# Attention and mixture of experts on one core: an emptying of GpSimd's queue in the last slot, and its halves multiplied and stored one by one

## The chip, the cores and the metric

The kernel runs on one core of a Trainium2 chip. The metric is the device time of one execution in microseconds, as the median of several runs; lower is better. The core has five engines that run side by side: TensorE (PE: matmuls, with its weight loads shown apart as PEld), VectorE (DVE), ScalarE (ACT), GpSimd (POOL) and SyncE (SP). They wait for each other through semaphores. An engine's name with a q (POOLq) stands for its sequencer, which issues, waits and branches.

## The reference, cut to what matters

Attention with rotary positions over 8 batches, 8 heads, 576 positions and 64 values a head gives 4608 tokens of 512 values. Each token then goes through the one expert of eight that its gate picks, and is scaled:

```python
x = attn_out.transpose(0, 2, 1, 3).reshape(N, D)            # N = 4608, D = 512
logits = x @ w_gate
e_idx = np.argmax(logits, axis=1)
probs = softmax(logits); gate_w = probs[np.arange(N), e_idx]
eom = 1.0 / (1.0 + np.exp(-(x @ w_output_gate)))
for e in range(E):                                          # E = 8
    mask = e_idx == e
    h = np.maximum(x[mask] @ w1[e], 0.0)                    # w1[e]: 512 x 1024
    ye = h @ w2[e]                                          # w2[e]: 1024 x 512
    out[mask] = gate_w[mask, None] * eom[mask, e, None] * ye
```

## The kernel before, in words

The first part computes the attention; the second (class `Moe`) does the experts. Tokens of one expert are gathered into *slots*. A slot has one expert and one or two *halves* of 128 tokens; `self.todo[s][0]` is the number of halves. The order of the slots is fixed when the program is built: full slots of two halves first, then slots of two halves and of one mixed. The last slot that always runs has two halves; some further slots stand in a branch (`tc.If`, L1237) that is taken only if the tokens need them, which they do not here.

`run` (L1225) calls `slot` (L1202) for each slot. `slot` has eight steps j. In steps 0 to 3, `first` (L1125) multiplies the tokens with a quarter of w1 (matmuls at L1121, or L1113 in a slot of one half), and ScalarE and VectorE turn the sums into the hidden rows `ht`, kept as a high and a low part (L1137, L1138). In steps 4 to 7, `second` (L1152) multiplies them with a quarter of w2 into one accumulator `py` a half (matmuls at L1163): for each of the two blocks f of a quarter it goes over the halves and makes three products (high x high, high x low, low x high). In every step, weights of later steps are loaded by SyncE (L1069) and split into a high and a low part (ScalarE L1078; VectorE L1080, now and then GpSimd). Step 6 gathers the tokens of the slot after the next (GpSimd, an indirect DMA, L1055). In step 7, `store` (L1166) scales `py` of half 0 on ScalarE (L1172) and that of half 1 on VectorE (L1174) into `y`, and GpSimd scatters each half to the token rows of `out` with an indirect DMA (L1175). For the last slots no later weights, tokens or turns are left to prepare, so in the last slot steps 4 to 7 hold nothing but `second` and `store`.

Each engine runs its instructions in the order in which the program names them; the framework adds the semaphore waits between instructions that touch the same memory. Two scatters both write to `out` at rows that are known only at run time, so each scatter waits until the one before it has landed.

Behind the last slot stands the branch: each engine loads the flag `used` (L1235) and jumps over the body (L1237), and GpSimd's INC_SWDGE_SEM (L1237) stands there too. At the end of the program (recorded under L1273, the line that opens the framework's context) SyncE waits for the semaphores of all engines and DMAs, each engine runs a DRAIN, and GpSimd gathers the others' answers and releases them. At the program's start (L1285) there is a DRAIN on each engine as well.

Of the kernel before, what the change touches and what calls it, by code (L numbers as in the profile page):

```python
# [10 lines left out]
F32 = mybir.dt.float32  # L11
# [3 lines left out]
AF = mybir.ActivationFunctionType  # L15
ALU = mybir.AluOpType
# [5 lines left out]
DM = H * D  # L22
E, FF = 8, 1024
P = 128
# [562 lines left out]
def place(tc, pools, pairs, b, NT, cc, trib, oneb, cnt, xbs, xd, row, lists, later):  # L587
# [173 lines left out]
    if last:  # L761
        later += [lambda i=i: store(i) for i in range(3)]
        run = lambda *fs: lambda: [f() for f in fs]
        return [s0, run(s1, s2), s3, run(s4, s5), run(s6, s7), run(s8, add0), both(s9, 1), lambda: [add(c) for c in (2, 3, 4)],
                run(s10, s11, s12), run(s13, base), no, no, no, no, s14, no, s14b, run(s15, s16, s17)] + [
                lambda c=c: (ones(c), places(c)) for c in range(NCH)] + [no, no, s20, no, s21, no]
# [12 lines left out]
    if b == NT // S - 2:  # L779
        later += [lambda i=i: store(i) for i in range(3)]  # L780
        fs += [(22, 2, s13)]
    else:
        fs += [(29, 2, lambda: gated(0, 2)), (33, 2, lambda: store(0)), (38, 2, lambda: gated(2, NCH)),
               (42, 2, lambda: store(1)), (42, 2, lambda: store(2))]
# [3 lines left out]
class Moe:  # L788
# [360 lines left out]
        self.nc.scalar.copy(hth[:, js, 0:P], tp[:, 0:2, :])  # L1149
        self.nc.vector.tensor_tensor(out=htl[:, js, 0:P], in0=tp[:, 0:2, :], in1=hth.bitcast(F32)[:, js, 0:P], op=ALU.subtract)  # L1150

    def second(self, s, j):  # L1152
        hth, htl = self.ht[s]
        K = self.todo[s][0]
        if j == 0:
            self.pys[s] = [self.pm.tile([P, DM], F32, tag=f"py{h}", name=f"py{s}_{h}{self.nm}") for h in range(K)]
        py = self.pys[s]
        for f in (2 * j, 2 * j + 1):
            wh, wl = (a.rearrange("p (f d) -> p f d", d=DM)[:, f % 2, :] for a in self.wp[8 * s + 4 + j])
            for h in range(K):  # L1160
                hs = slice(h * P, h * P + P)
                for n, (st, mv) in enumerate(((hth, wh), (hth, wl), (htl, wh))):
                    self.nc.tensor.matmul(py[h], st[:, f, hs], mv, start=(f == 0 and n == 0), stop=(f == 7 and n == 2))  # L1163
        self.wp.pop(8 * s + 4 + j)

    def store(self, s):  # L1166
        nc = self.nc
        py, gs = self.pys.pop(s), self.gss.pop(s)
        y = self.buf("y", s, 2, 0, [P, 2, DM], F32, f"y{s}{self.nm}")
        for h in range(self.todo[s][0]):  # L1170
            if h == 0:
                nc.scalar.activation(y[:, 0, :], py[0], AF.Copy, scale=gs[:, 0:1])  # L1172
            else:
                nc.vector.tensor_scalar(y[:, 1, :], py[1], gs[:, 1:2], None, op0=ALU.mult)  # L1174
            nc.gpsimd.indirect_dma_start(  # L1175
                out=self.out, out_offset=bass.IndirectOffsetOnAxis(ap=self.ids(s, h), axis=0),
                in_=y[:, h, :], in_offset=None, bounds_check=self.NT - 1, oob_is_err=False)

    LOADS, SPLITS, LEAD = 8, 9, 6

# [18 lines left out]
        for u in range(8 * s + 3, 8 * s + self.LEAD):  # L1199
            self.split(u)  # L1200

    def slot(self, s, left, per=2):  # L1202
        for j in range(8):
            u = 8 * s + j
            single = self.todo[s][0] == 1
            if j < 4:
                if s or j > 1 or not self.n0:
                    self.first(s, j)
            else:
                self.second(s, j - 4)  # L1210
            if single and 1 <= j <= 4:
                self.across(s, j - 1)
            self.split(u + self.LEAD)
            self.load(u + self.LOADS)
            if j in (4, 5):
                self.turn(s + 1, j - 4)
            if j == 7:
                self.store(s)
            if j == 6:
                self.gather(s + 2)  # L1220
            for _ in range(per if s or j > 1 else 1):
                if left:
                    left.pop(0)()

    def run(self, left):  # L1225
        left = list(left)
        N = self.end
        self.more(0)
        for s in range(N):
            self.slot(s, left)  # L1230
        while left:
            left.pop(0)()
        M = len(self.todo)
        if N < M:
            rv = self.nc.values_load(self.used[0:1, 0:1], min_val=0, max_val=self.n1,  # L1235
                                     skip_runtime_bounds_check_because="bounded by the number of tokens")
            with self.tc.If(rv > self.T):  # L1237
                self.begin0(N, M, "b")
                self.begin1(N)
                self.more(N)  # L1240
                for s in range(N, M):
                    self.slot(s, [])
# [46 lines left out]
```

## Time and profile before

| what | us |
|---|---|
| median of 3 runs (lowest, highest) | 986.09 (985.11, 987.06) |
| the profiled execution: its time | 985.03 |
| the profiled execution: span from first to last instruction | 983.3 |
| busy in the span: PE, DVE, ACT, POOL | 898.3, 759.7, 629.1, 563.4 |
| mean granted TensorE clock, share of full | 0.993 |

The times of the runs are what the change is judged by. The span is what the trace covers; all times of instructions below count from its start. Of the profiled execution's time, 1.7 us lie outside the span. A POOL row of DMA_INDIRECT is the issue of an indirect DMA, not its transfer; the transfer ends when it lands, which the chain of waits shows as DMA.

### The profile page before, as it was taken

To read this page: it belongs to the slowest core of one execution; us is meant where nothing else is said; L and a number is where in the kernel's file an instruction comes from. 1 tells how busy PE (TensorE), PEld (TensorE's weight loads), DVE (VectorE), ACT (ScalarE), POOL (GpSimd) and SP (SyncE) were. 2 spreads that over 40 slices of the span, in tenths; PEclk is the share of its full clock that TensorE was granted. 3 is DMA by queue.
4 is the path that set the end of the run, shared out by engine and by line. 5 is a ranking of instruction groups with operands and counts; after the bars stand their busy time and mean duration, and the time that the engine had idled before them with its cause. 6 is when DMAs were issued, how large, how long until landed. Compare 5 with 4: busy or idle time off the path is not lost.

```text
span 983.3 us, 34130 instructions
## 1 busy us (share of the span) xinstructions
PE 898.3 (91%) x14413; PEld 780.4 (79%) x14413; DVE 759.7 (77%) x1322; ACT 629.1 (64%) x1278; POOL 563.4 (57%) x565
## 2 busy tenths in 40 slices
PE   4989888988989888988899999999999999999993
PEld 3777777767777777776688989999899999988993
DVE  6889998998999999998779766557766766667560
ACT  4676787876878778686654544457656656565460
POOL 5787899999999999998411212142504234050410
PEclk9999999999999999999999999999999999999997
DMA  6543454564555456353589867667876869678630
GB/s 231 195 174 129 187 222 144 201 239 145 202 203 190 165 195 236 130 212 110 185 309 286 315 221 237 222 221 266 305 239 241 302 195 336 203 248 291 216 107 20
DMA packets 57822, 208.39 MB, mean 212 GB/s; under 512 B 7946, under 2 KB 8252, under 8 KB 57664
## 3 DMA queue, kind: packets, MB, share of 16 engines
q1 hardware_dynamic: 49920, 183.78, 53.7%
q0 software_dynamic: 6464, 21.26, 5.8%
q8 instruction: 115, 1.88, 0.8%
q10 hardware_dynamic: 1280, 1.11, 0.3%
q14 instruction: 43, 0.35, 0.1%
HBM read 186.06 MB, written 22.43 MB: 212 GB/s over the span
## 4 chain that ended last, share of the span: by engine, by line
PE 57%; DVE 14%; POOL 14%; issue 5%; ACT 4%; DMA 4%; SPq 0%; POOLq 0%; DVEq 0%; ACTq 0%
PE py L1163 18%; PE ph L1121 17%; PE acc L550 8%; PE sc L504 7%; DVE pm L513 6%; POOL raw L455 5%; DVE pt L528 4%; POOL kq L468 4%; PE ph L1113 3%; POOL raw L459 2%; ACT pm L520 2%; DVE xb L577 2%; PE mtp L1086 2%; DVE wl L1080 1%; POOL pl L738 1%
## 5 line engine op out<-in xcount | busy, mean ns | idle before, releaser
L520 ACT ACTIVATE pm<-pm,m 128x576 f32<-128x576 f32 x288 | 221.5, 770 | 96.2 <-DVE pm L513 94.2
L1080 DVE TENSOR_TENSOR wl<-wr,wh 128x1024 fp32r<-128x1024 f32 x172 | 216.0, 1270 | 37.5 <-ACT wh L1078 35.6
L513 DVE TENSOR_SCALAR_CACHE_REDUCE pm<-sc 128x576 f32<-128x576 f32 x288 | 207.7, 754 | 33.2 <-PE sc L504 26.1
L550 PE MATMUL acc<-pt,v 32*64 32x160 f32 (+1 forms) x9216 | 197.6, 295 | 18.6 <-DVE xb L577 6.9
L1163 PE MATMUL py<-wh,ht 128*128 128x512 f32 x640 | 213.1, 399 | 0.0
L1121 PE MATMUL ph<-xt,wh 128*128 128x256 f32 x1088 | 195.5, 282 | 0.5 <-DVE xt L1102 0.5
L550 PEld LDWEIGHTS acc<-pt,v 32*64 32x64 f32 x9216 | 157.4, 131 | 44.4 <-issue 22.0
L1078 ACT CAST wh<-wr 128x1024 fp32r<-128x1024 f32 x184 | 187.9, 1049 | 0.0
L528 DVE STREAM_TRANSPOSE pt<-pm 128x1152 f32<-128x1152 f32 x128 | 175.7, 1373 | 0.0
L1121 PEld LDWEIGHTS ph<-xt,wh 128*128 128x128 f32 x1088 | 167.8, 188 | 3.5 <-DVE xt L1102 2.2
L504 PE MATMUL sc<-kq 64*128 64x288 f32 x1536 | 149.8, 318 | 18.1 <-ACT kq L465 9.4
L455 POOL TENSOR_TENSOR raw<-raw,rt 128x1152 f32<-128x1152 f32 x62 | 164.3, 2651 | 0.6
L504 PEld LDWEIGHTS sc<-kq 64*128 64x128 f32 x1536 | 115.1, 190 | 47.7 <-issue 16.2
L1121 PE MATMUL ph<-xt,wl 128*128 128x256 f32 x544 | 152.8, 281 | 0.0
L1163 PEld LDWEIGHTS py<-wh,ht 128*128 128x128 f32 x640 | 120.3, 188 | 24.1
L1163 PE MATMUL py<-wl,ht 128*128 128x512 f32 x320 | 125.0, 391 | 0.0
L1175 POOL DMA_INDIRECT out<-y,2idx x24 | 28.2, 1174 | 168.3 <-ACT y L1172 122.8
L1137 ACT ACTIVATE ht<-ph 128x512 fp32r<-128x512 f32 x68 | 40.7, 598 | 108.7 <-PE ph L1121 108.7
L1121 PEld LDWEIGHTS ph<-xt,wl 128*128 128x128 f32 x544 | 102.5, 188 | 0.2
L1138 DVE SCALAR_TENSOR_TENSOR ht<-ph,ht 128x512 fp32r<-128x512 f32 x68 | 47.0, 691 | 69.1 <-ACT ht L1137 69.1
L468 POOL TENSOR_TENSOR kq<-raw,kq 128x1152 fp32r<-128x1152 f32 (+1 forms) x33 | 82.7, 2507 | 9.4 <-ACT kq L465 9.4
L459 POOL TENSOR_TENSOR raw<-raw 128x1152 f32<-128x1152 f32 (+1 forms) x33 | 82.5, 2499 | 1.8
(247 smaller groups left out, 1055.5 us busy)
## 6 DMA issues: line engine op xcount, KB each, us to landing
wr<-in_w SPq DMA_DIRECT2D x184, 512.0 KB, 4.9
raw<-in_qk SPq DMA_DIRECT2D x64, 576.0 KB, 4.9
v<-in_v SPq DMA_DIRECT2D x64, 576.0 KB, 6.8
xd<-xb SPq DMA_DIRECT2D x16, 640.0 KB, 4.4
xd<-xb SPq DMA_DIRECT2D x8, 160.0 KB, 5.0
rt<-in_rope ACTq DMA_DIRECT2D x1, 576.0 KB, 5.5
xg<-xd,2idx POOLq DMA_INDIRECT x24, 6.9
out<-y,2idx POOLq DMA_INDIRECT x24, 4.5
```

The costliest lines, as they stand in the source:

```text
L455: self.eng(eng).tensor_tensor(out=rv, in0=rv, in1=rt, op=ALU.mult)
L459: self.eng(eng).tensor_tensor(out=r, in0=r, in1=self.sides(self.raw, t, 1, x), op=ALU.add)
L468: self.eng(eng).tensor_tensor(out=self.sides(self.kq, t, 0, x), in0=self.sides(self.raw, t, 0, x), in1=self.sides(self.kq.bitcast(F32), t, ...
L504: self.nc.tensor.matmul(self.ps[i][:, a, :HS], st, self.kq[r, mov, x], start=(n == 0), stop=(n == 2))
L513: self.nc.vector.tensor_scalar(self.halves(i), self.ps[i][:, :, :HS], 1.0, FAR, op0=ALU.mult, op1=ALU.min, accum_out=self.m[i])
L520: self.nc.scalar.activation(self.pc[i], self.pc[i], AF.Exp, bias=self.m[i], scale=-1.0, accum_out=self.z[:, zi:zi + 1])
L528: self.nc.vector.transpose(out=self.pt[:, c:c + 6:5, :], in_=self.pc[units])
L550: nc.tensor.matmul(self.acc[h * D:h * D + D, a, o:o + 32 * n], self.v[r, h, j, :], self.pt[r, u:u + n, 32 * j:32 * j + 32], start=(j == 0) ...
L1078: self.nc.scalar.copy(wh, r)
L1080: eng.tensor_tensor(out=wl, in0=r, in1=wh.bitcast(F32), op=ALU.subtract)
L1121: nc.tensor.matmul(ph[:, f, :], st[:, dc, fs], mv[:, dc, :], start=(n == 0), stop=(n == 11))
L1163: self.nc.tensor.matmul(py[h], st[:, f, hs], mv, start=(f == 0 and n == 0), stop=(f == 7 and n == 2))
```

## The change

A method `close` takes the place of the last four calls of `second` and of `store` in the last slot that always runs: it makes all products of half 0 (all four quarters of w2), scales it on ScalarE and scatters it, then the same for half 1, also on ScalarE. `second` gets the list of halves to work on, and keeps the weights until `close` drops them. The second scatter of that slot is declared free of a dependence on the first. At the end of step 0 of the last slot, GpSimd gets a `drain` instruction. Other slots keep their order.

```diff
-    def second(self, s, j):
+    def second(self, s, j, halves=None):
...
-        if j == 0:
+        if s not in self.pys:
...
-            for h in range(K):
+            for h in range(K) if halves is None else halves:
...
-        self.wp.pop(8 * s + 4 + j)
+        if halves is None:
+            self.wp.pop(8 * s + 4 + j)
+
+    def scatter(self, s, h, y):
+        return self.nc.gpsimd.indirect_dma_start(
+            out=self.out, out_offset=bass.IndirectOffsetOnAxis(ap=self.ids(s, h), axis=0),
+            in_=y[:, h, :], in_offset=None, bounds_check=self.NT - 1, oob_is_err=False)
...
+    def close(self, s):
+
+        before = None
+        for h in range(self.todo[s][0]):
+            for j in range(4):
+                self.second(s, j, (h,))
+            if h == 0:
+                py, gs, y = self.pys[s], self.gss.pop(s), self.buf("y", s, 2, 0, [P, 2, DM], F32, f"y{s}{self.nm}")
+            self.nc.scalar.activation(y[:, h, :], py[h], AF.Copy, scale=gs[:, h:h + 1])
+            st = self.scatter(s, h, y)
+            if before is not None:
+                self.tc.declare_no_dep(st.ins, before.ins, reason="a token is in one half of one slot: the rows are others")
+            before = st
+        self.pys.pop(s)
+        for j in range(4):
+            self.wp.pop(8 * s + 4 + j)
...
-    def slot(self, s, left, per=2):
+    def slot(self, s, left, per=2, last=False):
...
-            else:
+            elif not last:
                 self.second(s, j - 4)
...
-                self.store(s)
+                self.close(s) if last else self.store(s)
             if j == 6:
                 self.gather(s + 2)
+            if j == 0 and last:
+                self.nc.gpsimd.drain()
...
-            self.slot(s, left)
+            self.slot(s, left, last=s == N - 1)
```

## Rows read from the trace of the kernel before

**Rows 1.** The page: engines' busy time; chain that ended last, by engine.

```profile
PE 898.3 (91%) x14413; PEld 780.4 (79%) x14413; DVE 759.7 (77%) x1322; ACT 629.1 (64%) x1278; POOL 563.4 (57%) x565
...
PE 57%; DVE 14%; POOL 14%; issue 5%; ACT 4%; DMA 4%; SPq 0%; POOLq 0%; DVEq 0%; ACTq 0%
```

**Rows 2.** Stretches: length, busy of PE PEld DVE ACT POOL, clock, DMA share, GB/s.

```profile
957.20:968.40 11.20, 11.19 (x50) 8.90 (x49) 0.69 (x1) 1.27 (x2) 0.00 (x0) 1.00 0.01 1
...
968.40:983.30 14.90, 0.00 (x0) 0.00 (x0) 0.75 (x1) 0.02 (x1) 1.96 (x2) 0.62 0.09 32
...
949.10:963.80 14.70, 14.70 (x101) 13.59 (x100) 5.22 (x6) 4.19 (x6) 0.00 (x0) 1.00 0.04 13
...
975.30:981.90 6.60, 0.00 (x0) 0.00 (x0) 0.00 (x0) 0.00 (x0) 0.00 (x0) 0.50 0.00 0
```

**Rows 3.** The chain that ended last, in order of time: start, us, what.

```profile
947.02 3.67 DMA out<-y,1idx
...
968.69 3.15 DMA out<-y,2idx
```

**Rows 4.** GpSimd in order of time, from 946: start, us, instruction, idle before.

```profile
947.02 2.06 POOL L1175 DMA_INDIRECT out<-y,1idx  x1 [7.42 <-ACT y L1172]
...
968.69 0.98 POOL L1175 DMA_INDIRECT out<-y,2idx  x1 [19.61 <-ACT y L1172]
...
972.62 0.98 POOL L1175 DMA_INDIRECT out<-y,2idx  x1 [2.94 <-DMA out<-y,2idx]
```

**Rows 5.** ScalarE and VectorE in order of time, last slot.

```profile
967.73 0.69 ACT L1172 ACTIVATE y<-py,gs 128x512 f32<-128x512 f32 x1 [9.66 <-PE py L1163]
...
953.40 1.22 DVE L1080 TENSOR_TENSOR wl<-wr,wh 128x1024 fp32r<-128x1024 f32 x1 [0.25 <-ACT wh L1078]
...
958.10 0.69 DVE L1138 SCALAR_TENSOR_TENSOR ht<-ph,ht 128x512 fp32r<-128x512 f32 x1 [2.13 <-ACT ht L1137]
...
968.42 0.75 DVE L1174 TENSOR_SCALAR y<-py,gs 128x512 f32<-128x512 f32 x1 [9.63 <-PE py L1163]
```

**Rows 6.** Line 1237 from 972: ns min/median/max, first and last start.

```profile
L1237 POOLq INC_SWDGE_SEM  x1: 1839/1839/1839, 973.3 to 973.3; - x1
```

**Rows 7.** The program's end, line 1273, by instruction: ns, first and last start.

```profile
L1273 SPq DRAIN  x2: 7/10/13, 975.8 to 975.9; - x2
...
L1273 POOLq DRAIN  x1: 6773/6773/6773, 975.2 to 975.2; - x1
...
L1273 POOLq EVENT_SEMAPHORE  x4: 17/17/17, 982.0 to 983.2; - x4
...
L1273 POOLq DRAIN  x2: 46/150/254, 982.5 to 983.0; - x2
...
L1273 DVEq DRAIN  x2: 10/14/17, 969.4 to 982.3; - x2
```

**Rows 8.** TensorE in order of time: a slot of one half, the last slot.

```profile
944.02 0.39 PE L1163 MATMUL py<-wl,ht 128*128 128x512 f32 x1
...
944.71 0.39 PE L1163 MATMUL py<-wl,ht 128*128 128x512 f32 x1
...
957.27 0.39 PE L1163 MATMUL py<-wh,ht 128*128 128x512 f32 x1
...
967.99 0.40 PE L1163 MATMUL py<-wh,ht 128*128 128x512 f32 x1
```

**Rows 9.** Scatters to out from 900 on: from issue to landing.

```profile
DMA to landing us min/median/max: 2.6/3.7/5.8
```

**Rows 10.** The program's start, line 1285, GpSimd's DRAIN.

```profile
L1285 POOLq DRAIN  x1: 184/184/184, 0.3 to 0.3; - x1
```

**Rows 11.** MOVEs, one ahead of each indirect DMA: scatters, gathers, index lists.

```profile
L1175 POOLq MOVE  x40: 29/29/29, 498.7 to 968.5; - x40
...
L1055 POOLq MOVE  x40: 29/29/38, 466.5 to 923.7; - x40
...
L857 POOLq MOVE  x2: 29/29/29, 549.4 to 596.3; - x2
```

More of the change, by code (lines that the diff above doesn't have):

```diff
@@ L1163, in second @@
                     self.nc.tensor.matmul(py[h], st[:, f, hs], mv, start=(f == 0 and n == 0), stop=(f == 7 and n == 2))
-        self.wp.pop(8 * s + 4 + j)
+        if halves is None:
[4 more added lines that the diff above has]
+            in_=y[:, h, :], in_offset=None, bounds_check=self.NT - 1, oob_is_err=False)
     def store(self, s):
-        nc = self.nc
         py, gs = self.pys.pop(s), self.gss.pop(s)
@@ L1171, in store @@
             if h == 0:
-                nc.scalar.activation(y[:, 0, :], py[0], AF.Copy, scale=gs[:, 0:1])
+                self.nc.scalar.activation(y[:, 0, :], py[0], AF.Copy, scale=gs[:, 0:1])
             else:
[L1174 to L1177, printed above, removed]
+                self.nc.vector.tensor_scalar(y[:, 1, :], py[1], gs[:, 1:2], None, op0=ALU.mult)
+            self.scatter(s, h, y)
+    def close(self, s):
[13 more added lines that the diff above has]
+            self.wp.pop(8 * s + 4 + j)
     LOADS, SPLITS, LEAD = 8, 9, 6
```

## The prediction

> **What bounds the kernel now.** I read the page first: TensorE is busy for most of the span and the chain that ended last runs mainly through it [rows 1], so what the change can win lies where TensorE no longer sets the pace. The table of stretches shows where that is [rows 2]: TensorE is full up to 968.4, the end of the last slot's second step, and does nothing in the last 14.9 us. From 975.3 to 981.9 no engine is busy and no DMA moves a byte. Next I read the tail. The chain of waits [rows 3] and GpSimd's order of time [rows 4] show that the first scatter of the last slot starts at 968.69, lands 3.15 us later, and only then the second starts, at 972.62, though its half was scaled by 969.17 [rows 5]. After it stands a fixed sequence on GpSimd: the skipped branch with INC_SWDGE_SEM, 1.84 us from 973.3 [rows 6], and a DRAIN from 975.2 that lasts 6.77 us [rows 7]. SyncE has its waits behind it at 975.9; GpSimd, which gathers the others at the end, first answers at 982.0 [rows 7]. So two things set the end: a wait of one scatter for the other, and a DRAIN that runs with every transfer landed.
>
> **The stores.** Step two of the last slot is 48 matmuls, whose starts run from 957.27 to 967.99 [rows 8]: 10.72 us over 47 gaps, 0.228 us each. The change keeps all 48 and puts the 24 of half 0 first. Does the new order stall TensorE? A slot of one half already puts its matmuls into one accumulator with no other half between, and starts three of them in 0.69 us there, 944.02 to 944.71 [rows 8], the same pace. The operands are needed earlier: those of the last weight unit at the 19th matmul instead of the 37th, so at 957.27 + 18 x 0.228 = 961.4 instead of 965.5. The last split of weights starts at 953.40 and takes 1.22 us, the last split of the hidden rows starts at 958.10 and takes 0.69 us [rows 5]: 954.6 and 958.8, 2.6 us before 961.4. The new order therefore costs nothing; without that cover TensorE would wait.
>
> Half 0 then ends at 957.27 + 23 x 0.228 + 0.40 = 962.9. ScalarE has nothing between 958.1 and 967.7 [rows 5], takes its 0.69 us and ends near 963.6; from ScalarE's end to the scatter it is 0.27 us now (968.42 to 968.69) [rows 4, 5], so scatter 0 starts near 963.9, 4.8 us earlier. It lands 2.6 to 5.8 us after its issue, median 3.7 [rows 9]: 966.5 to 969.7. Half 1 ends with TensorE at 968.39, as before. Its scaling moves from VectorE (0.75 us) to ScalarE (0.69 us), 968.43 to 969.12, and scatter 1 starts at 969.39 instead of 972.62: 3.23 us sooner. That the wait between the two is dropped is worth nothing at the median landing (967.6, 1.8 us early), and about 0.3 us of wait plus the 0.8 us from landing to scatter [rows 3, 4] if scatter 0 took the longest. What follows on GpSimd, SyncE's last waits included, hangs on scatter 1 and its landing and moves with it: **3.23 us**.
>
> **The emptying.** Where it stands, GpSimd has issued the scatter of 947.02, done at 949.08, and has nothing until the new scatter 0 [rows 4]: 14.8 us of cover. Only the two scatters are queued behind it, and nothing else waits for GpSimd in this slot. What does it do to the DRAIN at the end? Rows bound that one's later price. Below: a DRAIN with little or nothing ahead of it takes 0.18 us at the program's start and 0.05 to 0.25 us right behind the long one [rows 7, 10]. Above: 6.77 us, if the long one's price does not depend on what was emptied before. Between the ends stands an estimate: 82 indirect DMAs, 40 scatters, 40 gathers and 2 of index lists, are issued before it [rows 11], and (6.77 - 0.18) / 82 = 0.080 us each. I take this, because the long DRAIN outlasts every transfer, so it is work done on a list and not a wait for data, and the short ones stand where that list is empty. The new DRAIN in the slot then retires 80 of them, 0.18 + 80 x 0.080 = 6.6 us, from 949.1 to about 955.7, or until the scatter before it lands, 3.67 us after 947.02 [rows 3], whichever is later; 8.2 us remain before scatter 0. The last DRAIN has two left: 0.34 us. Then SyncE answers last, 0.7 us after the DRAIN starts (975.2 to 975.9) [rows 7], so a last DRAIN up to that length is free. GpSimd's answer moves from 982.0 to just behind 975.9, allowing 0.05 us for the signal: **6.05 us** more.
>
> **Sum.** 3.23 + 6.05 = 9.28 us. The profiled execution took 985.03 us for a span of 983.3, so its own time becomes 975.75. It lies 1.06 us under the median of the three runs shown, 986.09; against that the forecast is **976.8 us**. A measurement of this kernel tells apart about 0.2%, 2.0 us.
>
> **The rivals.** (1) *The price stays.* The last DRAIN costs 6.77 us whenever an indirect DMA ran before it, and the one in the slot is paid in the shade for nothing. Then only the stores gain: 986.09 - 3.23 = 982.9. For it: the trace has no second DRAIN behind an indirect DMA. Against: the transfers had landed before it began, so its length is not that of the last scatter. The Trainium skill, VectorE: DVE Perf Modes, section "The DRAIN you can't avoid", counts DRAINs around the program as boilerplate of a constant 12 ns or so on all five engines. By that rule there is nothing at the end to take away, and the sum would be that of the stores alone, 982.9. The trace agrees for SyncE and VectorE, 7 to 17 ns, and contradicts it for GpSimd, 6,773 ns [rows 7, 10].
>
> (2) *Part of the price stays*, since only the latest entries, or INC_SWDGE_SEM, carry it. Each microsecond of the last DRAIN beyond 0.7 gives one back: 976.8 to 982.9, middle 979.9.
>
> (3) *No change*: the 80 entries take much longer in the slot than at the end, and hold both scatters. Scatter 0 is late once the emptying exceeds 963.9 - 949.1 = 14.8 us; scatter 1 (at least 1.2 us behind, by scatter 0's 0.98 us [rows 4] and an issue) is late from 19.1 us, and the whole gain is gone at 28 us, 986.1. For it: GpSimd slows beside VectorE's splits, 2.06 us for a scatter at 947.02 against 0.98 later [rows 4]. Against: VectorE has only 5.2 us of work in that stretch [rows 2], and doubling the whole gives 13.2 us, still covered.
>
> (4) *Slower*: the emptying acts as a fence for all engines. TensorE then stands for its 6.6 us at the head of the slot, and if the last DRAIN stays too, the sum is 986.09 - 3.23 + 6.6 = 989.5. It decides for slower only when both hold; if the last one shrinks, it is 986.09 - 9.28 + 6.6 = 983.4. Against: the change adds one GpSimd instruction and no work of another engine that reads what GpSimd writes in this slot.
>
> That the change does not take the wait between scatters away at all would not show, as said: scatter 0 has mostly landed by then.
>
> **How the numbers follow.** The forecast has 0.65, the price that stays 0.15, a part of it 0.12 and the fence that still gains 0.01: faster 0.93. Rival 3 and other ways to land within 0.2% have 0.04, slower 0.03. The likeliest case alone spans 975.4 to 978.5: the runs shown scatter by 1 us either way, and 0.7 us lies on the last landing (2.6 or 3.2 us). The range reaches to the rival that keeps the price, with half a microsecond: 975.4 to 983.4, leaving out some 5% below and about 11% above.
>
> **What the profile after should show.** A DRAIN on GpSimd of 6 to 7 us from about 949; scatter 0 near 963.9 and scatter 1 near 969.4, with no wait for a landing between; two scalings of 0.69 us on ScalarE; TensorE still ending near 968.4; a last DRAIN under 0.7 us and a span near 974.0. The prediction is wrong if the last DRAIN is again several microseconds long, if the one in the slot lasts past 963.9, or if TensorE stops between 957 and 968.

## The result and the profile after

The changed kernel takes 977.13 us (median of 4 runs, 976.42 to 978.65) against 985.63 us beside it. The ratio is 0.9914 with a 95% interval of 0.9896 to 0.9931: 8.5 us less, 6.8 to 10.3. The forecast was 976.8 us, 9.28 us under the kernel before.

The profiled execution is the slowest of the four (978.65 us, span 976.9), and TensorE ends in it at 970.93, 2.5 us later than before [rows 8]. Those 2.5 us are lost far ahead of the change, on the way from the attention to the slots, where this execution has a stretch with the clock at its lower level (1.2 GHz). (Columns: length, busy time of PE, PEld, DVE, ACT and POOL with instruction counts, granted clock, DMA share, GB/s.)

```profile
470.00:520.00 50.00, 44.45 (x725) 39.14 (x724) 32.97 (x64) 29.62 (x54) 11.65 (x24) 0.93 0.59 215
```

A mean clock of 0.93 over 50 us is what 7 us at the lower level make. TensorE had been busy for all of the 5 us before the clock fell (470 to 475) and for 3.00 of the 5 us in which it fell. None of the seven experiments' executions below shows it there (1.00 in each). So kernels are compared here by their *tail* too: from the end of the last matmul to the end of the span. It was 983.3 - 968.39 = 14.9 us and is 976.9 - 970.93 = 6.0 us.

GpSimd in order of time (start, length, instruction, idle time before it and what ended it), to be held against [rows 4]:

```profile
949.50 2.06 POOL L1168 DMA_INDIRECT out<-y,1idx  x1 [7.41 <-ACT y L1177]
...
966.40 0.98 POOL L1168 DMA_INDIRECT out<-y,2idx  x1 [14.85 <-ACT y L1190]
...
971.93 0.98 POOL L1168 DMA_INDIRECT out<-y,2idx  x1 [4.54 <-ACT y L1190]
```

Scatter 0 starts 4.53 us before TensorE's end and scatter 1 1.00 us behind it, where it was 4.23 us; what released it is ScalarE's scaling and no longer a landing. ScalarE, against [rows 5]:

```profile
965.44 0.69 ACT L1190 ACTIVATE y<-py,gs 128x512 f32<-128x512 f32 x1 [4.91 <-PE py L1163]
...
970.97 0.69 ACT L1190 ACTIVATE y<-py,gs 128x512 f32<-128x512 f32 x1 [4.84 <-PE py L1163]
```

TensorE's second step of the last slot, first and last matmul; then three stretches around the emptying and the end (columns as above):

```profile
959.73 0.40 PE L1163 MATMUL py<-wh,ht 128*128 128x512 f32 x1
...
970.53 0.40 PE L1163 MATMUL py<-wh,ht 128*128 128x512 f32 x1
```

```profile
949.30:958.20 8.90, 8.90 (x78) 8.90 (x77) 5.68 (x7) 3.67 (x5) 2.06 (x1) 1.00 0.05 20
...
958.20:970.90 12.70, 12.70 (x63) 10.36 (x61) 0.93 (x2) 1.28 (x2) 0.98 (x1) 1.00 0.06 23
...
970.90:976.90 6.00, 0.03 (x1) 0.00 (x0) 0.00 (x0) 0.69 (x1) 0.98 (x1) 0.74 0.10 37
```

The 48 matmuls still take 10.80 us from first start to last, against 10.72, and TensorE is busy in every microsecond from the emptying's start to its own end: 8.90 of 8.90 and 12.70 of 12.70. So the emptying is no fence. The instructions of the emptying (line 1242), of the skipped branch (1259) and of the program's end (1295), against [rows 6, 7] (ns min/median/max, first and last start in us):

```profile
L1242 POOLq DRAIN  x1: 8903/8903/8903, 949.3 to 949.3; - x1
...
L1259 POOLq INC_SWDGE_SEM  x1: 246/246/246, 972.6 to 972.6; - x1
...
L1295 SPq EVENT_SEMAPHORE  x14: 17/28/2003, 972.8 to 976.8; - x14
...
L1295 POOLq EVENT_SEMAPHORE  x4: 17/17/17, 975.6 to 976.8; - x4
...
L1295 POOLq DRAIN  x3: 52/261/2148, 972.9 to 976.6; - x3
```

The last scatter, from issue to landing:

```profile
L1168 POOL DMA_INDIRECT out<-y,2idx x1: 982/982/982, 971.9 to 971.9; - x1
...
DMA to landing us min/median/max: 3.0/3.0/3.0
```

The DRAIN in the slot is recorded from 949.3, ahead of the scatter of 949.50 that stands before it, and ends at 958.2: 6.6 us behind the end of that scatter's issue. At the program's end two rows have shrunk, not one: the last DRAIN from 6,773 to 2,148 ns and INC_SWDGE_SEM from 1,839 to 246 ns. SyncE now stands 2,003 ns in one of its waits, for the last scatter's landing, and has its last waits behind that. The last DRAIN, too, ends only at 975.0, just behind the landing (971.9 + 3.0 = 974.9). GpSimd answers at 975.6, 3.7 us behind the issue of scatter 1, where it was 9.4 us.

### The profile page after: what moved, and what is told of

It is laid out like the page before. It is cut to its first block, busy times and chain, and to the rows that moved or that the text cites. A ratio compares the mean times of both kernels' runs of the same rounds, so it can differ in the third digit from the quotient of the medians.

```text
span 976.9 us, 34128 instructions
## 1 busy us (share of the span) xinstructions
PE 899.7 (92%) x14413; PEld 782.2 (80%) x14413; DVE 759.0 (78%) x1321; ACT 629.7 (64%) x1279; POOL 559.4 (57%) x565
## 4 chain that ended last, share of the span: by engine, by line
PE 56%; POOL 19%; DVE 12%; issue 6%; DMA 3%; ACT 3%; POOLq 0%; SPq 0%; DVEq 0%; ACTq 0%
PE py L1163 18%; PE ph L1121 18%; PE acc L550 7%; POOL raw L455 7%; PE sc L504 6%; DVE pm L513 5%; POOL kq L468 5%; PE ph L1113 3%; DVE pt L528 3%; POOL raw L459 2%; POOL pl L738 2%; PE mtp L1086 2%; DVE xb L577 1%; DMA raw<-in_qk 1%; DVE wl L1080 1%
## 5 line engine op out<-in xcount | busy, mean ns | idle before, releaser
L565 PE MATMUL acc<-ii,ac 128*128 128x160 f32 x320 | 54.3, 319 | 32.4 <-ACT ac L559 32.4
```

The source lines that it names most:

```text
L565: self.nc.tensor.matmul(flat[:, BS * c:BS * c + BW], self.ac[:, c, :, :].rearrange("p a x -> p (a x)"), self.ii[:, self.hp, :], start=True ...
```

## The experiments

Theory: a DRAIN of GpSimd works off a list of the indirect DMAs since the last one (each of them an *entry*), at some 0.08 us each, so an emptying under cover takes that price off the end. Rival: the price is fixed, per DRAIN or once. Diffs are against the changed kernel. Those of the first four ran together (the kernel before: 986.15 us, 15 runs), the last three too (985.33 us, 12 runs).

### The emptying alone

```diff
-            elif not last:
+            else:
                 self.second(s, j - 4)
...
-                self.close(s) if last else self.store(s)
+                self.store(s)
```

> The emptying alone: the last slot keeps its old order and its old store. List theory (the DRAIN pays some 0.08 us for each indirect DMA since the last emptying): a DRAIN of 6 to 7 us behind the scatter ahead of the last slot, the last DRAIN down to what the last landing still needs (under 2.5 us), from TensorE's end to the end of the span 14.9 - 6.05 = 8.8 us, time 6 us under the kernel before. Rival, the price is the same whenever an indirect DMA ran: the last DRAIN stays near 6.8 us, no change of time.

979.63 us, ratio 0.9941 (0.9919 to 0.9962). GpSimd's two last scatters in order of time, then its DRAINs in the slot and at the end:

```profile
968.49 0.99 POOL L1168 DMA_INDIRECT out<-y,2idx  x1 [19.73 <-ACT y L1177]
...
972.41 0.99 POOL L1168 DMA_INDIRECT out<-y,2idx  x1 [2.93 <-DMA out<-y,2idx]
```

```profile
L1242 POOLq DRAIN  x1: 8910/8910/8910, 946.5 to 946.5; - x1
...
L1295 POOLq DRAIN  x3: 52/173/1754, 973.4 to 976.6; - x3
```

The scatters stand as before, the second behind the landing of the first. The last DRAIN fell from 6.77 to 1.75 us. TensorE ended at 968.18, so the tail is 976.9 - 968.18 = 8.7 us, 6.2 less than before; 8.8 us were expected. The fixed price is refuted.

### The halves one by one, without the emptying

```diff
-            if j == 0 and last:
-                self.nc.gpsimd.drain()
```

> The halves one by one and no wait between their scatters, without the emptying. By my sum: scatter 1 starts 1.0 us after TensorE's end instead of 4.2, the last DRAIN stays at 6.6 to 6.8 us, from TensorE's end to the span's end 14.9 - 3.2 = 11.6 us, time 3.2 us under the kernel before. Rival, the stores bring nothing because the DRAIN takes back what they save (its list is worked off from a fixed point): 14.9 us and no change. INC_SWDGE_SEM, 1.84 us before and 0.25 us after the change: if it is the emptying that shortens it, it is 1.8 us here.

983.54 us, ratio 0.996 (0.9943 to 0.9978). The second scatter, then INC_SWDGE_SEM and the last DRAINs:

```profile
972.71 0.98 POOL L1168 DMA_INDIRECT out<-y,2idx  x1 [4.54 <-ACT y L1190]
```

```profile
L1257 POOLq INC_SWDGE_SEM  x1: 1839/1839/1839, 973.4 to 973.4; - x1
...
L1293 POOLq DRAIN  x3: 46/107/6773, 975.3 to 982.9; - x3
```

TensorE ended at 971.71 in this execution, so scatter 1 starts 1.0 us behind it, and the tail is 983.2 - 971.71 = 11.5 us, 3.4 less than before; 11.6 were expected. DRAIN and INC_SWDGE_SEM are to the nanosecond what they were [rows 6, 7], so the emptying shortens both, and the stores neither. The two parts' tails sum to 6.2 + 3.4 = 9.6 us; together they give 8.9. Some 0.4 us of the difference is the last landing, for which the end waits once the list has been emptied: it came 2.6 us after its issue with the emptying alone and 3.0 us in the changed kernel.

### The wait between the scatters kept

```diff
-        before = None
...
-            st = self.scatter(s, h, y)
-            if before is not None:
-                self.tc.declare_no_dep(st.ins, before.ins, reason="a token is in one half of one slot: the rows are others")
-            before = st
+            self.scatter(s, h, y)
```

> The whole change, but the second scatter of the last slot keeps its wait for the first one's landing. By my sum scatter 0 lands 2.6 to 5.8 us after its issue, with 5.5 us between the two issues, so the wait is over before half 1 is scaled: the same time as the changed kernel within its noise, scatter 1 starting 1.0 us after TensorE's end. Rival, the dropped wait is what brings the stores' 3.2 us: scatter 1 starts 3 us later and the time is 3.2 us over the changed kernel.

976.87 us, ratio 0.9908 (0.9882 to 0.9934): the changed kernel's time. The two scatters:

```profile
965.46 0.99 POOL L1168 DMA_INDIRECT out<-y,2idx  x1 [16.07 <-ACT y L1189]
...
970.99 0.98 POOL L1168 DMA_INDIRECT out<-y,2idx  x1 [4.54 <-ACT y L1189]
```

TensorE ended at 969.99: scatter 1 again 1.00 us behind it, released by ScalarE, tail 5.7 us. The order of the halves brings the stores' gain alone; the dropped wait brings nothing here, since scatter 0 landed 4.6 us after its issue, at 970.1, and half 1 was scaled at 970.7.

### The emptying between the two scatters

```diff
             st = self.scatter(s, h, y)
+            if h == 0:
+                self.nc.gpsimd.drain()
...
-            if j == 0 and last:
-                self.nc.gpsimd.drain()
```

> The emptying moved behind scatter 0, between the two scatters, where its cover is short. List theory with 81 indirect DMAs on the list: 81 x 0.0826 = 6.7 us from the end of scatter 0's issue, so scatter 1 starts some 7 us after scatter 0's issue ends, 3.3 us after TensorE's end instead of 1.0: some 2.3 us over the changed kernel; the last DRAIN again waits for the landing alone. Rival, the DRAIN only waits for transfers in flight (here scatter 0's, 2 to 3 us): scatter 1 is not late, the last DRAIN is as long as it was, 6.8 us.

978.46 us, ratio 0.9922 (0.9902 to 0.9941). The two scatters, and the DRAIN:

```profile
963.28 0.98 POOL L1168 DMA_INDIRECT out<-y,2idx  x1 [14.86 <-ACT y L1190]
...
972.04 0.98 POOL L1168 DMA_INDIRECT out<-y,2idx  x1 [7.77 <-issue]
```

```profile
L1193 POOLq DRAIN  x1: 8177/8177/8177, 963.0 to 963.0; - x1
```

Scatter 0, from issue to landing:

```profile
L1168 POOL DMA_INDIRECT out<-y,2idx x1: 982/982/982, 963.3 to 963.3; - x1
...
DMA to landing us min/median/max: 4.6/4.6/4.6
```

The DRAIN ends 6.9 us behind the end of scatter 0's issue (963.0 + 8.2 = 971.2, against 964.26), and scatter 1 starts 0.8 us later, 4.2 us behind TensorE's end at 967.81 instead of 1.0; 3.3 were expected. The tail is 8.8 us, 2.8 over the changed kernel's, where 2.3 were expected. Its median is 1.6 us over that of the kernel with the wait kept, which the intervals do not part, so that the cover is needed rests on the scatter's place and the tail of one execution. Without full cover the price returns in part only, since TensorE still covers some 3.5 us of it.

### The emptying at the head of slot 1

```diff
-            if j == 0 and last:
+            if j == 0 and s == 1 and not self.nm:
```

> The emptying moved to the head of slot 1, where 8 indirect DMAs are on the list (2 scatters, 6 gathers); the halves of the last slot stay one by one. List theory: the DRAIN there works off 8 x 0.083 = 0.7 us after the last issue (or waits for that one's landing), and the last DRAIN still has 74 entries, 6.1 us; from TensorE's end to the span's end 10.8 us, time 5 us over the changed kernel. Rival, the first DRAIN behind an indirect DMA pays a fixed 6.6 us once (something that has to be fetched or set up), later ones do not: 6.6 us in slot 1 and a last DRAIN under 2.2 us, 5.7 to 6 us from TensorE's end.

981.77 us, ratio 0.9962 (0.995 to 0.9974). The DRAIN in slot 1; the scatter before it and its landing; INC_SWDGE_SEM; the DRAINs at the end:

```profile
L1242 POOLq DRAIN  x1: 6104/6104/6104, 524.4 to 524.4; - x1
...
L1168 POOL DMA_INDIRECT out<-y,0idx x1: 986/986/986, 524.7 to 524.7; - x1
...
DMA to landing us min/median/max: 5.5/5.5/5.5
...
L1259 POOLq INC_SWDGE_SEM  x1: 1679/1679/1679, 971.3 to 971.3; - x1
...
L1295 POOLq DRAIN  x3: 52/254/6102, 973.0 to 980.1; - x3
```

The last DRAIN is 6,102 ns and the tail 980.4 - 969.61 = 10.8 us, as the list had it. A price paid once at a first DRAIN is refuted. The DRAIN in slot 1 is long only in the record: its scatter, issued at 524.7, landed 5.5 us later at 530.2, and the DRAIN ended at 530.5.

### The emptying at the head of slot 12

The same line with `s == 12`.

> The emptying moved to the head of slot 12 of 23, with 49 indirect DMAs ahead of it and 33 behind. List theory: 49 x 0.083 = 4.0 us behind the last issue there, 33 x 0.083 = 2.7 us at the end; from TensorE's end to the span's end 5.7 us if INC_SWDGE_SEM is short (0.25 us) and 7.5 us if it is 1.84 us as in the kernel before. Rival, the price of the last DRAIN is all or nothing (6.6 us, or the landing alone): 11.5 or 5.7 us.

977.35 us, ratio 0.9919 (0.9901 to 0.9937). Rows as above:

```profile
L1242 POOLq DRAIN  x1: 8605/8605/8605, 760.4 to 760.4; - x1
...
L1168 POOL DMA_INDIRECT out<-y,2idx x1: 1659/1659/1659, 760.7 to 760.7; - x1
...
DMA to landing us min/median/max: 6.3/6.3/6.3
...
L1259 POOLq INC_SWDGE_SEM  x1: 859/859/859, 970.9 to 970.9; - x1
...
L1295 POOLq DRAIN  x3: 52/255/2920, 971.8 to 975.8; - x3
```

The last DRAIN is 2,920 ns for 33 entries, INC_SWDGE_SEM 859 ns, and the tail 976.0 - 969.24 = 6.8 us: the middle that all or nothing excludes, and between the 5.7 and 7.5 us that were expected for a short and a long INC_SWDGE_SEM. In the slot the theory is off: 4.0 us were expected behind the end of the issue at 762.3, and it took 6.7 us, to 769.0. The scatter before it landed at 760.7 + 6.3 = 767.0, so 2.0 us of the DRAIN came behind the landing. TensorE is busy for 50.00 of the 50 us from 750 to 800, so this stayed covered.

### Two emptyings

```diff
-            if j == 0 and last:
+            if j == 0 and (last or s == 12):
```

> Two emptyings, at the head of slot 12 and of the last slot. List theory: 4.0 us at slot 12, then 31 x 0.083 = 2.6 us at the last slot instead of 6.6 us, counted from the end of the issue ahead of it (or until that one has landed), the end as in the changed kernel (5.7 to 6 us from TensorE's end) and the same time. Rival, a DRAIN costs the same 6.6 us each time an indirect DMA ran before it: 6.6 us twice.

976.81 us, ratio 0.9928 (0.9904 to 0.9952). The DRAINs in the slots; the scatter ahead of each and its landing; the DRAINs at the end:

```profile
L1242 POOLq DRAIN  x2: 5212/6803/8394, 759.5 to 945.8; - x2
...
L1168 POOL DMA_INDIRECT out<-y,2idx x1: 1011/1011/1011, 759.8 to 759.8; - x1
...
DMA to landing us min/median/max: 6.1/6.1/6.1
...
L1168 POOL DMA_INDIRECT out<-y,1idx x1: 2058/2058/2058, 946.0 to 946.0; - x1
...
DMA to landing us min/median/max: 3.7/3.7/3.7
...
L1295 POOLq DRAIN  x3: 52/173/2304, 969.4 to 973.2; - x3
```

The second DRAIN starts at 945.8, takes 5,212 ns and ends at 951.0, 2.9 us behind the end of the issue at 948.1: near the 2.6 us that 31 entries were to take, and not the 6.6 us that 80 take at the same place. The rival's same price each time is refuted. The first DRAIN, at slot 12, is again longer than the 4.0 us that were expected: it ends at 767.9, 7.2 us behind the end of the issue, but again 2.0 us behind the landing at 765.9. The end is that of the changed kernel (tail 973.5 - 967.45 = 6.0 us).

### The list, measured

| kernel | entries at the end | INC_SWDGE_SEM, ns | last DRAIN, ns |
|---|---|---|---|
| before; halves only | 82 | 1,839 | 6,773 |
| emptied at slot 1 | 74 | 1,679 | 6,102 |
| emptied at slot 12 | 33 | 859 | 2,920 |
| changed kernel | 2 | 246 | 2,148 (waits for the landing) |

The upper three DRAINs lie on 0.33 us + 0.0783 us an entry, within 0.03 us, and the four INC_SWDGE_SEM on 0.20 us + 0.020 us an entry, to a few ns. The first line gives 0.33 + 80 x 0.0783 = 6.6 us for the DRAIN in the last slot, as measured. The DRAIN with 33 entries is not free of its landing, though (last section); the two above it give 0.084 us an entry by themselves.

The number of entries and the time that has passed rise together in these kernels. INC_SWDGE_SEM parts them: 8 and 41 fewer entries take 160 and 820 ns off, 20.0 ns an entry both times. The time since the first entry or the last emptying falls by some 66 and 240 us, 2.4 and 3.4 ns a us, so it is the number that counts. Every scatter and gather here moves 128 rows, so no run shows whether the price goes by DMA or by row.

## Why the prediction was right, point by point

**The stores: right.** Scatter 0 was forecast 4.5 us ahead of TensorE's end and came 4.53 ahead; scatter 1 was forecast 1.00 us behind it and came 1.00 behind. The new order cost TensorE nothing (10.80 against 10.72 us from first to last start). That the dropped wait is worth nothing was forecast for the median landing, and the kernel that keeps it shows it.

**The emptying in the slot: right.** 6.6 us were forecast and 6.6 us measured from the end of the scatter's issue; 8.2 us remained before scatter 0, as forecast (958.2 to 966.4).

**The last DRAIN: right in mechanism, wrong in size.** 0.34 us was forecast, 2.15 us measured. That is three times the 0.7 us up to which it was to be free, and near the sign of being wrong that the prediction named ("several microseconds"). The two entries cost little, but the DRAIN also stands until the last scatter has landed. The prediction had left INC_SWDGE_SEM at 1.84 us, as part of a fixed sequence that only moves; behind it the landing would have been over. It is not fixed: it is another price of the list, 0.020 us an entry, and fell to 0.25 us. The two errors cancel, by luck as far as the prediction goes: SyncE's waits hang on the same landing and end later (GpSimd has its answer at 975.6) than the DRAIN (975.0), so the DRAIN's extra length costs nothing. From the issue of scatter 1 to GpSimd's answer the forecast had 3.3 us (975.95 - 972.62), and 3.7 us were measured; the difference is that landing, 3.0 us in this execution against 2.6 before (the smallest of [rows 9]).

**The sum.** The tail fell by 8.9 us where 9.28 were forecast; the medians fell by 8.5 with an interval that holds both.

**The rivals.** That the price stays is refuted by the emptying alone. That part of it hangs on INC_SWDGE_SEM is true of 1.6 us in the kernel before, but the emptying takes them away as well. A slow emptying was the right thing to fear: at slot 12 it took 2.7 us longer than expected, not from work of VectorE beside it, where the prediction looked, but behind a late landing (2.0 us behind it in both kernels that empty there; last section), and stayed covered; moved to where TensorE covers only part of it, it cost 2.8 us of tail. The fence did not happen. The Trainium skill's rule of a constant 12 ns or so for DRAINs around a program (VectorE: DVE Perf Modes, "The DRAIN you can't avoid") fits the other engines here, 7 to 17 ns [rows 7]; GpSimd's goes by the number of its indirect DMAs, 2,920 to 6,773 ns for 33 to 82.

## What to carry to other kernels

Read the tail of the span by itself: rows of the sequencers that no table of busy time counts, such as a DRAIN while no engine and no DMA works, are on the path to the end. In this kernel the many indirect DMAs that GpSimd issues leave a price that falls due at the end unless a DRAIN is put where GpSimd idles anyway; so look for a long DRAIN of GpSimd at the end of such kernels. Place the emptying late, so that few entries follow, with cover for the later of two times: some 0.08 us an entry from the end of the last issue, and 0.04 us an entry from the newest landing. And bring work forward rather than drop a wait: once half 0 is finished 5.5 us ahead of half 1, a landing 4.6 us after its issue is over before anyone waits for it.

## What the runs showed of the hardware that was not expected

INC_SWDGE_SEM is no fixed cost: 31 ns at the program's start, then 246, 859, 1,679 and 1,839 ns with 2, 33, 74 and 82 indirect DMAs since the last emptying.

A DRAIN behind a scatter that lands late does part of its work only after the landing. The last scatter of the kernel emptied at slot 12, whose last DRAIN ends at 974.7:

```profile
L1168 POOL DMA_INDIRECT out<-y,2idx x1: 982/982/982, 970.2 to 970.2; - x1
...
DMA to landing us min/median/max: 3.1/3.1/3.1
```

From the newest landing to the DRAIN's end, to 0.01 us from the traces (the rows shown give tenths):

| entries | where | us behind the landing |
|---|---|---|
| 1 | end, emptied between the scatters | 0.09 |
| 2 | end, changed kernel | 0.13 |
| 8 | slot 1 | 0.38 |
| 31 | last slot, two emptyings | 1.31 |
| 33 | end, emptied at slot 12 | 1.40 |
| 49 | slot 12, in both kernels that empty there | 2.06 |
| 81 | between the scatters | 3.36 |

All lie on 0.05 us + 0.041 us an entry, within 0.01 us: half of the 0.084 us that an entry costs where the landing is over long before the DRAIN ends. So the misses at slot 12 and between the scatters are one effect: a DRAIN ends at the later of two times, one counted from its start or the last issue and one from the newest landing. That reads like two passes over the list, one that can run ahead of the landing and one that cannot; no run shows the passes themselves, so this reading stays open.
